# Loading 120 rows in place of 128 for the last matmul of an FFT convolution

## The chip, the cores and the metric

The kernel runs on one core of a Trainium2 chip. The metric is the device time of one execution in microseconds (us). The kernel before took 1574.06 us (median of 3 runs, 1570.44 to 1580.28).

## The reference

Two stages. The first convolves `u = x*v` (4 batches, 11456 positions, 128 channels) causally with a filter that a small network makes of position embeddings, and multiplies the outcome by `x`. The second sends each of the 45824 rows to one of 8 experts of two layers (128 to 1024 to 128), if a score of the row is above zero.

```
u = x * v
Uf = np.fft.rfft(u, n=L, axis=1)
Hf = np.fft.rfft(h_filt, n=L, axis=0)
y = np.fft.irfft(Uf * Hf[None, :, :], n=L, axis=1)[:, :S, :]
return (x * y).astype(np.float32)
...
e_idx = np.argmax(logits, axis=1)
...
    h = np.maximum(xc[mask] @ w1[e], 0.0)
    y[mask] = gate_w[mask, None] * (h @ w2[e])
out[do_compute] = xc + y
```

## The kernel before

The transform of length 3840 is split as 60 x 64 (`K1` = 60, `N2` = 64) and is done with matmuls in fp32 in three phases, one after the other in each engine's program.

- `first_phase` and `freq_phase`: the first takes the transform over 60 points (lines 209 and 211; its outcome is stored to DRAM from 120 partitions, line 197) and builds the filter (`filt`, line 257). The second takes the transform over 64 points (`spread`, L395), multiplies by the filter on VectorE and GpSimd, goes back over 64 points (`backer`, L430, 433) and stores the outcome `z` to the DRAM tensor `zd` (line 442). In `zd` each of the 32 output chunks has 2*`K1` = 120 rows (60 real, 60 imaginary) for either parity `p`, with 4 heads of 384 values (1536 bytes) each. Behind the last chunk lie 8 rows of zeros (`ZR`, line 1397), so that 128 rows can be read from every chunk.
- `out_phase`: for chunk `ch` and parity `p`, `load_z` reads rows of `zd` into the tile `zt` (two buffers, `ZB`). `load_z` is called from `produced` and, for the first two chunks, ahead of the loop, where the last head is loaded apart, as it is stored last. `product` multiplies `zt` by the table `c4`, for each of three blocks of a chunk: two matmuls (one for each `p`, into 64 PSUM partitions each) with 512 columns, then a product with `x` on VectorE (L1129). A matmul in fp32 stands as two instructions in the trace, so 32 x 3 x 2 products are 384 matmul instructions. The table's rows from 120 on are zero.
- The rest of `out_phase` decides for each row which expert it goes to, and the experts' work (`early_slots`, lines 735 to 825, afterwards `late_slots`) is put between the steps by a fixed order: the program's order on every engine is written out when it is built, and nothing of it depends on when a transfer lands.

The queues that matter: SP (SyncE) issues the loads of `zt` (L1109), of `x` (L1100, tile `ox`) and of `c4` (L1098) and the stores of the chunks (L1133), all in program order. ACT issues the stores of line 197 and the last twelve of line 442. GpSimd issues the indirect gathers and scatters of the experts.

Of the kernel before, what the change touches and what calls it, by code (L numbers as in the profile page):

```python
# [22 lines left out]
K1, N2 = 60, 64  # L23
# [4 lines left out]
NP = 4  # L28
# [25 lines left out]
C4 = 2  # L54
# [1000 lines left out]
def out_phase(tc, i, out, zd, ex, consts):  # L1055
# [3 lines left out]
    nc = tc.nc  # L1059
    NT = NS  # L1060
    NCH = H2
    with (
# [3 lines left out]
      with (  # L1066
# [23 lines left out]
        zs = zd.rearrange("p h r w -> r (p h) w")  # L1090
        c4s, xms, zx, zts, lgs = {}, {}, {}, {}, {}
# [11 lines left out]
        def load_z(ch, p, heads=slice(0, NP)):  # L1103

            if ch < NCH:
                if ch not in zts:
                    zts[ch] = oz.tile([128, 2 * NP, NS * DH], F32, name="zt")
                rows = slice(p * NP + heads.start, p * NP + heads.stop)
                nc.sync.dma_start(zts[ch][:, rows], zs[2 * K1 * ch:2 * K1 * ch + 128, rows])  # L1109

        def load(q, x=None):

# [7 lines left out]
        def product(ch, blk):  # L1120
            z, x = zx.pop(NB * ch + blk)
            if blk == 0:
                xms[ch] = ob.tile([128, NS, W], F32, name="xm", bufs=XM)
            xm = xms[ch]
            s = slice(blk * B, (blk + 1) * B)
            y = opy.tile([128, NP, B, DH], F32, name="y")
            for p in range(2):
                nc.tensor.matmul(y[p * 64:(p + 1) * 64], c4s[ch // C4][:, ch % C4, p, :], z[:, NP * p:NP * (p + 1)], start=True, stop=True)  # L1128
            nc.vector.tensor_tensor(xm[:, s, 0:D].rearrange("p b (h d) -> p h b d", h=NP), y, x, ALU.mult)  # L1129

        def store(ch, blk):
# [158 lines left out]
        for p in range(2):  # L1290
            load_z(0, p, most)
        ahead = [load_x(q) for q in range(ZT - 1)]
        for p in range(2):
            load_z(1, p, most)
        for ch in range(2):
            for p in range(2):
                load_z(ch, p, last)
# [37 lines left out]
        def produced(ch, blk):  # L1335
            product(ch, blk)
            load(NB * ch + blk + ZT - 1)

            if blk == NB - 1:
                load_z(ch + ZB, 0)  # L1340
            elif blk == 0 and ch > 0:
                load_z(ch + 1, 1)
# [128 lines left out]
```

## Time and profile before

| | us |
|---|---|
| median of 3 runs | 1574.06 |
| the profiled execution | 1575.11 |
| span of its instructions | 1573.2 |
| TensorE busy | 1485.4 |
| VectorE busy | 1057.4 |
| GpSimd busy | 963.8 |
| ScalarE busy | 790.3 |

Busy time is the time in which an engine had an instruction in work. A matmul's end is modelled in the profile, so that a busy TensorE is not TensorE at its peak. The granted clock is the share of TensorE's full speed that the chip allowed. The DMA share is the mean busy share of the core's 16 DMA engines; it can come out a little above 1. "Idle before" names the instruction or transfer that ended an engine's wait, "issue" a wait that nothing in the profile explains.

### The profile page before, as it was taken

The numbers are of one execution on the slowest core, as the hardware profiler recorded it, in microseconds if no ns is written. First come the engines' busy times: TensorE is split into PE (matmuls) and PEld (weight loads), VectorE is DVE, ScalarE is ACT, GpSimd is POOL, SyncE is SP. The second block draws the span as 40 slices with busy tenths as digits, with TensorE's granted clock in tenths as the row PEclk, the third lists the DMA queues.
The fourth block names the chain that finished last, engine by engine and source line by source line (L and its number), as shares of the span: only waits on it lengthen the run. The fifth ranks groups of instructions, "written<-read, shape, count | busy, mean of one in ns | idle before, by whom it ended". The sixth has DMA issues, their size and how long they took to land. (4 is left out here: it accounts for less than half of the span.)

```text
span 1573.2 us, 27965 instructions
## 1 busy us (share of the span) xinstructions
PE 1485.4 (94%) x9149; PEld 906.7 (58%) x9149; DVE 1057.4 (67%) x2356; ACT 790.3 (50%) x1643; POOL 963.8 (61%) x808
## 2 busy tenths in 40 slices
PE   6994999999999999978899999999979999999997
PEld 2552344444444444424477667666667788888887
DVE  1322776777777798856876666676658677777773
ACT  4552555555555544424355544544535455555554
POOL 0101876777777666621466369528856678888765
PEclk9996999999999999989899999999999999999999
DMA  8999999999999989969977687777521111111100
GB/s 319 316 335 339 364 390 371 377 360 363 359 390 361 301 230 359 316 218 344 314 237 227 218 240 243 246 233 234 152 57 39 36 46 45 46 45 44 41 28 24
DMA packets 199256, 362.18 MB, mean 230 GB/s; under 512 B 64476, under 2 KB 138730, under 8 KB 199070
## 3 DMA queue, kind: packets, MB, share of 16 engines
q1 hardware_dynamic: 173430, 272.15, 51.2%
q10 hardware_dynamic: 10192, 52.51, 9.1%
q0 software_dynamic: 15488, 35.74, 8.1%
q8 instruction: 73, 1.20, 0.3%
q14 instruction: 73, 0.60, 0.1%
HBM read 216.89 MB, written 145.42 MB: 230 GB/s over the span
## 5 line engine op out<-in xcount | busy, mean ns | idle before, releaser
L741 POOL DMA_INDIRECT out<-o,ids x182 | 197.7, 1086 | 158.2 <-DVE o L748 121.4
L488 POOL TENSOR_TENSOR y<-y,p 128x1536 f32<-128x1536 f32 x59 | 203.6, 3451 | 99.3 <-DVE p L415 99.3
L430 PE MATMUL ps<-y,c 64*128 64x256 f32 (+1 forms) x1440 | 259.2, 490 | 4.1 <-ACT wf L211 2.6
L670 POOL DMA_INDIRECT xt<-out,ids x182 | 189.6, 1042 | 48.1 <-issue 28.2
L883 DVE SCALAR_TENSOR_TENSOR hh<-hp,hh 128x1024 fp32r<-128x1024 f32 (+1 forms) x124 | 150.0, 1210 | 84.3 <-ACT hh L882 75.5
L430 PEld LDWEIGHTS ps<-y,c 64*128 64x128 f32 x1440 | 138.9, 187 | 117.3 <-issue 83.0
L399 ACT COPY xx<-xp 128x480 f32<-128x480 f32 x240 | 112.9, 523 | 129.2 <-PE xp L395 97.5
L882 ACT ACTIVATE hh<-hp 128x1024 fp32r<-128x1024 f32 (+1 forms) x124 | 127.6, 1029 | 94.7 <-issue 50.5
L433 ACT COPY z<-ps 128x512 f32<-128x512 f32 x240 | 103.7, 482 | 138.7 <-PE ps L430 127.2
L415 DVE TENSOR_TENSOR p<-xp,xx 128x768 f32<-128x768 f32 x240 | 169.3, 747 | 0.0
L415 DVE TENSOR_TENSOR y<-xp,xx 128x1152 f32<-128x1152 f32 x120 | 162.8, 1357 | 4.1
L406 DVE TENSOR_TENSOR xx<-xp,xx 128x384 f32<-128x384 f32 x120 | 66.7, 556 | 128.6 <-ACT xx L399 128.6
L395 PE MATMUL xp<-x,wf 128*64 128x480 f32 x512 | 120.9, 595 | 19.4 <-DMA x<-x1d 15.9
L1128 PE MATMUL y<-zt,c 128*64 128x512 f32 x384 | 109.2, 634 | 18.2 <-issue 10.5
L825 PEld LDWEIGHTS bank<-wd,h 128*128 128x128 f32 x896 | 104.2, 191 | 32.8 <-issue 25.9
L643 POOL MEMSET idle<- 128x512 f16 x226 | 122.5, 542 | 0.3
L209 PE MATMUL ps<-wf,c 60*120 60x384 f32 x512 | 119.4, 530 | 3.2 <-DVE wf L192 2.7
L211 ACT COPY wf<-ps 120x384 f32<-120x384 f32 x256 | 111.2, 499 | 21.6 <-PE ps L209 12.6
L192 POOL TENSOR_TENSOR wf<-wf 124x768 f32<-124x768 f32 x45 | 81.9, 1819 | 65.1 <-DVE xx L406 35.2
L621 POOL DMA_INDIRECT lists<-pl,lies x32 | 51.4, 1605 | 114.3 <-DVE step L1226 52.6
L825 PE MATMUL bank<-wd,h 128*128 128x128 f32 x896 | 114.5, 281 | 1.3 <-DVE o L748 1.3
L1129 DVE TENSOR_TENSOR xm<-y,ox 128x512 f32<-128x512 f32 x96 | 66.2, 689 | 69.1 <-PE y L1128 51.1
(180 smaller groups left out, 2934.3 us busy)
## 6 DMA issues: line engine op xcount, KB each, us to landing
wf<-xv SPq DMA_DIRECT2D x64, 768.0 KB
x1d<-wf ACTq DMA_DIRECT2D x64, 720.0 KB
x<-x1d SPq DMA_DIRECT2D x60, 768.0 KB
zt<-zd SPq DMA_DIRECT2D x60, 768.0 KB
zd<-z SPq DMA_DIRECT2D x108, 384.0 KB
out<-xm SPq DMA_DIRECT2D x96, 258.0 KB
ox<-xo SPq DMA_DIRECT2D x96, 256.0 KB
x1f<-fx POOLq DMA_DIRECT2D x16, 720.0 KB
```

The costliest lines, as they stand in the source:

```text
L209: nc.tensor.matmul(ps[p], self.c1[rows], u[rows, q * RUN:(q + 1) * RUN], start=True, stop=True)
L395: nc.tensor.matmul(xp[p * 64:(p + 1) * 64, c, 0:(NS + NB) * DH], c2(n % PER * KS + k)[:, c * 64:(c + 1) * 64], x1[:, k], start=True, stop= ...
L399: nc.scalar.copy(xx[:, 2 * c, 0:w], xp[:, c, 0:w])
L415: nc.vector.tensor_tensor(o[:, :, j].rearrange("p v m b d -> p v (m b) d"), v[:, :, None, s * DH:(s + 1) * DH].broadcast_to([128, NV, m, DH]),
L430: nc.tensor.matmul(zps[p], c3[r, v], yv[r, v, :, lo:hi], start=(v == 0), stop=(v == NV - 1))
L488: nc.gpsimd.tensor_tensor(y[:, :, :, 1:], y[:, :, :, 1:], p1, ALU.add)
L643: self.nc.gpsimd.memset(self.idle, 0.0)
L670: ins = nc.gpsimd.indirect_dma_start(out=xt[:, j], out_offset=None, in_=self.rows[0:have], in_offset=bass.IndirectOffsetOnAxis(ap=ids[:, j ...
L741: ins = nc.gpsimd.indirect_dma_start(out=self.rows, out_offset=bass.IndirectOffsetOnAxis(ap=ids[:, j:j + 1], axis=0), in_=o, in_offset=Non ...
L825: nc.tensor.matmul(bank[:, j * D:(j + 1) * D], h[f // nf][:, k:k + 128], wd[u][:, f * D:(f + 1) * D], start=(f == 0), stop=(f == F // 128 ...
L882: nc.scalar.activation(v[:, 0], hp, AF.Relu)
L883: nc.vector.scalar_tensor_tensor(v[:, 1], hp, 0.0, v[:, 0].bitcast(F32), ALU.max, ALU.subtract)
```

## The change

`load_z` reads 120 rows for each chunk into partitions 0 to 119 of `zt`, and both operands of the product are cut to partitions 0 to 119. The tile keeps its 128 partitions, and the table is still loaded whole.

```
-                nc.sync.dma_start(zts[ch][:, rows], zs[2 * K1 * ch:2 * K1 * ch + 128, rows])
+                nc.sync.dma_start(zts[ch][0:2 * K1, rows], zs[2 * K1 * ch:2 * K1 * (ch + 1), rows])
...
-                nc.tensor.matmul(y[p * 64:(p + 1) * 64], c4s[ch // C4][:, ch % C4, p, :], z[:, NP * p:NP * (p + 1)], start=True, stop=True)
+                nc.tensor.matmul(y[p * 64:(p + 1) * 64], c4s[ch // C4][0:2 * K1, ch % C4, p, :], z[0:2 * K1, NP * p:NP * (p + 1)], start=True, stop=True)
```

## Rows read from the trace of the kernel before

**Rows 1.** The page's 40 slices of the span, busy share in tenths.

```profile
PE   6994999999999999978899999999979999999997
DMA  8999999999999989969977687777521111111100
```

**Rows 2.** Stretches: length, busy PE, PEld, DVE, ACT, POOL; clock, DMA share, GB/s.

```profile
680.00:720.00 40.00, 27.36 (x163) 11.63 (x165) 19.06 (x42) 9.72 (x28) 2.55 (x2) 0.83 0.81 278
720.00:760.00 40.00, 33.94 (x315) 16.24 (x315) 31.94 (x136) 15.82 (x57) 6.40 (x6) 1.00 1.03 353
760.00:800.00 40.00, 35.23 (x295) 22.45 (x293) 29.83 (x120) 17.89 (x50) 22.34 (x27) 0.87 0.85 263
800.00:1128.00 328.00, 323.95 (x2757) 226.33 (x2750) 217.17 (x828) 161.17 (x421) 214.78 (x255) 1.00 0.75 233
```

**Rows 3.** Waits from 690 to 1140 us: us in total, times, longest.

```profile
PE y L1128 <- issue: 10.5, 2, 9.8
PEld y L1128 <- DMA zt<-zd: 1.9, 3, 1.0
DVE xm L1129 <- DMA zt<-zd: 2.7, 1, 2.7
SPq L1109 <- DMA zd<-z: 12.6, 3, 9.8
```

**Rows 4.** Timeline where the out phase begins: start, us, instruction, [idle before].

```profile
689.95 1.78 ACTq L442 DMA_DIRECT2D zd<-z  x2
...
696.64 2.04 SPq L1109 DMA_DIRECT2D zt<-zd  x4
...
699.04 2.35 PE L1128 MATMUL y<-zt,c 128*64 128x512 f32 x3 [9.84 <-issue]
```

**Rows 5.** Matmuls by line: ns min/median/max, first and last start, a form.

```profile
L430 PE MATMUL ps<-y,c x1440: 373/587/790, 164.3 to 688.8; 64*128 64x512 f32 x120, 64*128 64x256 f32 x60
...
L257 PE MATMUL ps<-hw,cf x160: 587/589/687, 35.1 to 116.9; 64*120 64x512 f32 x160
...
L209 PE MATMUL ps<-wf,c x512: 480/483/993, 11.2 to 537.7; 60*120 60x384 f32 x171
...
L1128 PE MATMUL y<-zt,c x384: 592/643/1116, 699.0 to 1128.0; 128*64 128x512 f32 x192
```

**Rows 6.** Timeline of TensorE: how closely matmuls of a line follow each other.

```profile
301.58 2.74 PE L430 MATMUL ps<-y,c 64*128 64x512 f32 x12
...
306.01 0.91 PE L209 MATMUL ps<-wf,c 60*120 60x384 f32 x4
...
709.94 1.08 PE L1128 MATMUL y<-zt,c 128*64 128x512 f32 x4
```

**Rows 7.** DMA issues of two lines: ns min/median/max of the issuing instruction.

```profile
L1109 SPq DMA_DIRECT2D zt<-zd x68: 333/426/1220, 679.0 to 1101.9; - x68
...
L197 ACTq DMA_DIRECT2D x1d<-wf x64: 322/323/730, 15.8 to 539.3; - x64
```

**Rows 8.** DMA from 680 to 760 us: packets and volume, then issues with KB each.

```profile
DMA packets 14869, 25.23 MB, mean 315 GB/s; under 512 B 1207, under 2 KB 9911, under 8 KB 14861
...
zt<-zd SPq DMA_DIRECT2D x13, 768.0 KB
...
zt<-zd SPq DMA_DIRECT2D x3, 576.0 KB
zt<-zd SPq DMA_DIRECT2D x4, 192.0 KB
```

**Rows 9.** DMA from 720 to 1128 us: packets and volume, then the issues of zt.

```profile
DMA packets 69218, 101.22 MB, mean 248 GB/s; under 512 B 13976, under 2 KB 44826, under 8 KB 69165
...
zt<-zd SPq DMA_DIRECT2D x56, 768.0 KB
```

**Rows 10.** DMA from 200 to 500 us: engines' share, then ACT's queue (line 197).

```profile
200.00:500.00 300.00, 296.75 (x1542) 127.68 (x1544) 221.74 (x317) 167.51 (x392) 230.25 (x98) 0.99 1.01 371
...
q10 hardware_dynamic: 4724, 25.81, 21.7%
```

## The prediction

> **What bounds the kernel now.** I read the slices first: TensorE is busy nine tenths or more nearly everywhere, and the DMA engines are full only up to the middle of the span [rows 1]. The change touches line 1109 and the two matmuls of line 1128, and the latter run only from 699 to 1128 us [rows 5], so I cut that part into stretches [rows 2]. The reader should see two different regimes there. From 800 to 1128 us TensorE is busy 323.95 of 328 us with the DMA engines at 0.75: work of the experts fills every gap, and TensorE sets the pace. From 720 to 760 us, before the experts' work begins, TensorE is busy 33.94 of 40 us and the DMA engines stand at 1.03: transfers have nothing to spare. From 680 to 720 us the phase begins, with 12.6 us of idle TensorE.
>
> Next, who really waits for the loads of z? From 690 to 1140 us TensorE's weight loads waited 1.9 us for them and VectorE 2.7 us, 4.6 us together [rows 3]. The one long wait is at the start: the last stores of z were issued from 689.95 us on, SP issued the loads of the last head at 696.64 us, and the first product followed at 699.04 us after 9.84 us of idleness [rows 4]. SP's longest wait there, 9.8 us, was for a store of z to land [rows 3]. That wait is for a store, whose size does not change.
>
> **The change part by part.** It removes rows 120 to 127 of each load, one sixteenth of 64 x 768 KB = 50.3 MB, that is 3.15 MB. It moves nothing in any program: the same loads and matmuls are issued in the same order, with the same waits, so nothing new is queued behind anything on SP or elsewhere.
>
> *Matmuls.* 384 instructions contract 120 rows instead of 128, still over 512 columns. No row shows 120 rows, so I take the nearest on both sides. With 64 rows, 256 columns take at least 373 ns (the minimum of line 430 is that of its smaller form) and 512 columns 587 ns (line 257): 214/256 = 0.836 ns per column. The matmuls of line 209 contract only 60 rows over 384 columns: the line gives 373 + 128 x 0.836 = 480 ns, and the minimum is 480. With 128 rows and 512 columns line 1128 takes 592 ns against 587 with 64 [rows 5]. So time goes by columns, and rows have no price: 0 us. If it went by rows, one sixteenth of 384 x 0.592 us would be 14 us, but line 209 would then be far below its line. The bound above comes from how closely matmuls follow each other. Twelve of line 430 take 2.74 us, (2.74 - 0.587)/11 = 0.196 us apart; four of line 1128 take 1.08 us, (1.08 - 0.592)/3 = 0.163 us apart; four of line 209, (0.91 - 0.480)/3 = 0.143 us for 384 columns, or 0.191 scaled to 512 [rows 6]. If cutting the rows took line 1128 from the spacing of a full column of the array to that of the partial ones, it would cost 384 x 0.033 = 12.7 us, all on the path, since TensorE is full. I take 0: those two lines also load 120 and 128 weight columns where line 1128 loads 64, which explains them as well. Weight loads have the same 64 columns: 0.
>
> *Issue on SP.* 68 instructions of 333 ns at least (426 in the median) [rows 7]. The stores of line 197 already have 120 rows and are issued in 322 to 323 ns [rows 7]. So 0; SP has time between issues anyway.
>
> *Transfers.* How much sooner does a load land? Upper bound of the gain: every byte saved is time saved. At the 353 GB/s of the full stretch [rows 2], 3.15 MB are 8.9 us over the whole phase. But a saving counts only where transfers hold something up. In 680 to 760 us z makes 13 x 768 + 3 x 576 + 4 x 192 = 12480 KB = 12.8 MB of 25.2 MB [rows 8]; a sixteenth is 0.80 MB, 2.3 us. Behind 800 us TensorE covers it, and what was waited for in all is 4.6 us [rows 3]. At the start the four loads of the first heads run ahead of the last store: a sixteenth of 4 x 576 KB is 0.15 MB, 0.4 us. So the likely gain lies between 0 and some 2 us if the saving is shared by all engines, with the ceiling at 8.9. Lower bound (a loss): loads that take longer in their new form, the third rival below. I take 0: 120 rows can be spread as 15 engines with 8 rows each, and then the engines that do work carry exactly what each of 16 carried for 128 rows, and only one is relieved. The nearest row for this form: line 197's 120-row stores, on ACT's queue, took 21.7% of engine time for 25.81 of 111.32 MB (23%: 371 GB/s x 300 us), with all engines at 1.01 [rows 10]. The form costs no more per byte than the rest and leaves no engine idle for long.
>
> [...]
>
> **Sum.** 0 (matmuls) + 0 (issue) + 0 (transfers) = 0. The profiled execution took 1575.11 us, 1.05 us above the median of the runs, so the sum is 1575.1 against that execution, and 1574 against the median.
>
> **The rivals.**
>
> *Saved bytes count everywhere.* Transfers follow the volume, and the full stretch and the start shrink: -2.3 - 0.4 us, about 1571; at the ceiling 1565. For: 1.03 in 720 to 760 us. Against: only 4.6 us of waits on z, and engine-wise nothing is saved. Chance 0.11.
>
> *Matmuls follow each other less closely.* +12.7 us, 1587. For: the spacing of lines 209 and 430. Against: the durations, which know no rows. Chance 0.05.
>
> *Loads of 120 rows run slower* (slower than before). The place is the stretch from 704 to 760 us: z is 12.8/25.2 = 51% of its volume, and the engines are full. A load that takes f times as long costs 56 x 0.51 x (f - 1) us: with f = 1.3 that is 8.6 us, and it decides (1%, 15.7 us) from f = 1.55 on; with 1.6 it gives 1591. Beyond 800 us z is 56 x 768 KB = 44.0 of 101.2 MB [rows 9], an estimated 0.33 of the engines' time at 0.75; this stays hidden until f = 1.76. Against: line 197's price per byte; but those are stores, and no row shows a load into 120 partitions. Chance 0.06.
>
> *The split uses only 8 engines* (120 = 8 x 15). From 720 to 1128 us the DMA share is (40 x 1.03 + 40 x 0.85 + 328 x 0.75)/408 = 0.79; z is 0.435 of it by volume [rows 9], 0.34, the rest 0.45. On half the engines z would be 0.34 x 15/16 x 2 = 0.64, together 1.09: 408 us become 445, +37 us, 1611. Against: the engines at 1.01 with 21.7% of their time in 120-row stores [rows 10]; on 8 engines these would have left the other 8 idle for twice that share. Chance 0.03.
>
> *The change does less than it says*, for instance since 128 rows' worth of work stays: the same time as the forecast.
>
> **How the numbers follow.** The forecast, within some 5 us of no change, has 0.72; the last 0.03 are for the clock. [...] The prediction is 1574. About 1% (15.7 us) is what a measurement of this kernel can tell from no change. Faster by over 1%, under 1558, needs more than the ceiling of saved bytes: 0.04, for what I don't see. Slower by over 1%, over 1590: slow loads (0.05), 8 engines (0.03), spacing with something on top (0.03), the rest (0.01): 0.12. Within 1%: 0.84. The range goes from the ceiling of the saving, 1565, to the bound of the spacing and of f near 1.5, 1588.
>
> **What would show it.** Right: line 1128 still at 592 ns at least and 0.163 us apart, with 120 rows in its form; zt with 720 KB per issue and waits on it of a few us; the DMA share from 800 to 1128 us down by a sixteenth of z's part, 0.02; TensorE's stretch from 800 us on as long as before. Wrong by the rivals: fewer idle us from 700 to 760 and an earlier last line 1128 (bytes); 1.21 us for four matmuls (spacing); long waits of line 1128 on zt from 704 to 760 us (slow loads), or everywhere (8 engines). If the time moves by over 1% and none of these rows moved, my reading of what bounds the phase is wrong.

## The result and the profile after

The changed kernel is slower: 1592.85 us (median of 6 runs) against 1577.77 us for the kernel before in runs beside it, ratio 1.0135 with a 95% interval of 1.0111 to 1.0159. This ratio is the one on record; the quotient of the two medians is 1.0096, so the size of the loss is known less closely than the interval says. The forecast was 1574 us and no change, with a range up to 1588. The profiled execution took 1593.7 us, its span 1591.9, 18.7 us more than that of before.

The programs of the engines are the same but for the form of lines 1109 and 1128. So the first question is when the time is lost. The timeline gives the moment at which VectorE multiplies the first block of each chunk (line 1129):

| chunk | before, us | after, us | after is late by |
|---|---|---|---|
| 0 | 702.4 | 704.8 | 2.5 |
| 3 | 724.7 | 733.4 | 8.7 |
| 5 | 742.1 | 756.4 | 14.3 |
| 7 | 761.4 | 781.7 | 20.3 |
| 9 | 788.8 | 811.3 | 22.5 |
| 15 | 879.0 | 901.6 | 22.6 |
| 31 | 1119.1 | 1141.5 | 22.4 |

The lines behind the row of chunk 9, before first:

```profile
788.77 0.69 DVE L1129 TENSOR_TENSOR xm<-y,ox 128x512 f32<-128x512 f32 x1 [2.81 <-PE y L1128]
```

```profile
811.26 0.69 DVE L1129 TENSOR_TENSOR xm<-y,ox 128x512 f32<-128x512 f32 x1 [2.81 <-PE y L1128]
```

All of it is lost up to chunk 9, and from there on not a tenth of a microsecond per chunk. Behind chunk 31, 3.7 us are won back; where, I did not follow. The stretches of the changed kernel (length, busy time of PE, PEld, DVE, ACT, POOL, clock, DMA share, GB/s), to be held against [rows 2]:

```profile
680.00:720.00 40.00, 25.27 (x137) 10.54 (x133) 16.87 (x35) 8.96 (x25) 3.67 (x3) 0.79 0.84 227
720.00:760.00 40.00, 32.58 (x234) 14.79 (x235) 22.34 (x87) 11.71 (x41) 2.97 (x3) 0.79 1.04 264
760.00:800.00 40.00, 28.52 (x230) 13.41 (x229) 26.58 (x120) 12.10 (x41) 15.83 (x19) 0.83 0.99 254
800.00:1100.00 300.00, 294.44 (x2508) 206.11 (x2509) 200.57 (x761) 149.75 (x389) 179.11 (x212) 0.99 0.91 229
```

From 720 to 760 us the DMA engines are as full as before (1.04), but they move 264 GB/s in place of 353. From 800 us on they are busy 0.91 of the time for 229 GB/s. The same stretch of the kernel before, and the share of SP's queue (packets, MB, share of the engines) in both, before first and after second:

```profile
800.00:1100.00 300.00, 296.47 (x2531) 207.57 (x2524) 199.31 (x754) 148.38 (x387) 189.43 (x224) 1.00 0.76 238
...
q1 hardware_dynamic: 44761, 64.44, 66.4%
```

```profile
q1 hardware_dynamic: 42580, 62.44, 81.2%
```

Fewer bytes take more engine time: 62.44 MB in 81.2% against 64.44 MB in 66.4%. If the 14.8% of 300 us, 44 us, are all put down to z, whose part before was some 0.33 x 300 = 99 us by volume, then z takes 143 us where a sixteenth less would be 93: an estimated 1.5 times as long per byte. The packets in the two traces say it directly: on SP's queue those of z are the ones of 1536 bytes, and from 800 to 1100 us one took 78.7 ns in the mean before and 115.5 after (1.47 times), from 704 to 800 us 74.9 and 113.6 (1.52 times). That is hidden here, as TensorE is busy 294.44 of 300 us; it is not hidden up to chunk 9.

The transfers of 680 to 760 us, for [rows 8], and waits for transfers from 690 to 1160 us, for [rows 3]:

```profile
DMA packets 11263, 19.65 MB, mean 246 GB/s; under 512 B 880, under 2 KB 7530, under 8 KB 11257
...
zt<-zd SPq DMA_DIRECT2D x10, 720.0 KB
```

```profile
PE y L1128 <- DMA c<-c: 3.0, 1, 3.0
...
PEld y L1128 <- DMA zt<-zd: 4.0, 4, 1.5
...
DVE xm L1129 <- DMA ox<-xo: 5.7, 4, 2.2
```

In the same 80 us, 10 whole loads of z are issued instead of 13, and now line 1128 waits 3.0 us for the table c4 too, and VectorE 5.7 us for x: other loads are late too. Most of the new waiting stands as "issue", for which the profile names no releaser. Line 1128 has the following from 704 to 812 us, where the kernel before had 2.6 us of weight loads and 0.7 us of matmuls waiting so; that these are waits for loads is inferred from l_alone below:

```profile
PEld y L1128 <- issue: 15.2, 9, 5.0
PE y L1128 <- issue: 13.7, 4, 4.7
```

And the matmuls themselves (min/median/max in ns, then a group of four from the timeline), for [rows 5] and [rows 6]:

```profile
L1128 PE MATMUL y<-zt,c x384: 592/643/1117, 701.1 to 1150.4; 120*64 120x512 f32 x192
```

```profile
889.75 1.08 PE L1128 MATMUL y<-zt,c 120*64 120x512 f32 x4
```

592 ns and 1.08 us for four: not a nanosecond has changed.

### The profile page after: what moved, and what is told of

It reads as the page before. It is cut to its first block, busy times and chain, and to the rows that moved or that the text cites. A ratio compares the mean times of both kernels' runs of the same rounds, so it can differ in the third digit from the quotient of the medians.

```text
span 1591.9 us, 27965 instructions
## 1 busy us (share of the span) xinstructions
PE 1490.7 (94%) x9149; PEld 906.2 (57%) x9149; DVE 1058.3 (66%) x2356; ACT 790.7 (50%) x1643; POOL 964.2 (61%) x808
## 5 line engine op out<-in xcount | busy, mean ns | idle before, releaser
L399 ACT COPY xx<-xp 128x480 f32<-128x480 f32 x240 | 112.9, 523 | 129.9 <-PE xp L395 96.9
L1128 PE MATMUL y<-zt,c 120*64 120x512 f32 x384 | 117.0, 668 | 30.4 <-issue 25.0
L395 PE MATMUL xp<-x,wf 128*64 128x480 f32 x512 | 120.9, 595 | 18.4 <-DMA x<-x1d 14.8
L825 PEld LDWEIGHTS bank<-wd,h 128*128 128x128 f32 x896 | 104.2, 191 | 32.8 <-issue 25.9
```

The lines of the kernel that those rows point to most:

```text
L395: nc.tensor.matmul(xp[p * 64:(p + 1) * 64, c, 0:(NS + NB) * DH], c2(n % PER * KS + k)[:, c * 64:(c + 1) * 64], x1[:, k], start=True, stop= ...
L825: nc.tensor.matmul(bank[:, j * D:(j + 1) * D], h[f // nf][:, k:k + 128], wd[u][:, f * D:(f + 1) * D], start=(f == 0), stop=(f == F // 128 ...
L1128: nc.tensor.matmul(y[p * 64:(p + 1) * 64], c4s[ch // C4][0:2 * K1, ch % C4, p, :], z[0:2 * K1, NP * p:NP * (p + 1)], start=True, stop=True)
```

## The experiments

Each ratio is against the kernel before on the same chip, with a 95% interval. "Chunk 0 to 9" is the time from the first product of chunk 0 to that of chunk 9, 86.4 us before and 106.4 us after; in five kernels whose early loads of z and x go into all 128 partitions (before, m_alone, z_heads, late120, store128) it lies between 86.4 and 90.0 us, so a single profile tells differences from some 4 us on.

| run | what is different from before | ratio | chunk 0 to 9, us |
|---|---|---|---|
| changed kernel | 120 rows loaded and contracted | 1.0135 (1.0111 to 1.0159) | 106.4 |
| m_alone | 120 rows contracted only | 1.0029 (1.0000 to 1.0058) | 90.0 |
| l_alone | 120 rows loaded only | 1.0152 (1.0106 to 1.0197) | 103.5 |
| late120 | 120 rows loaded from chunk 10 on, contracted in all | 0.9993 (0.9971 to 1.0014) | 87.9 |
| halves | z in two loads of 64 partitions | 1.0154 (1.0090 to 1.0219) | 107.6 |
| z_heads | z in two loads of half the heads | 1.0007 (0.9984 to 1.0030) | 88.4 |
| x_halves | x in two loads of 64 partitions | 1.0046 (1.0020 to 1.0071) | 96.3 |
| out_halves | output in two stores of 64 partitions | 1.0010 (0.9973 to 1.0046) | 91.2 |
| r112p8 | 120 rows as 112 and 8 | 1.0119 (1.0072 to 1.0165) | 102.2 |
| r112 | 112 rows only | one run | 96.9 |
| r96 | 96 rows only | one run | 104.9 |
| half_z | half of the heads from chunk 2 on | one run | 84.5 |
| mid64 | partitions 32 to 95 from chunk 2 on | one run | 84.0 |
| low64 | partitions 0 to 63 from chunk 2 on | one run | 85.8 |
| store128 | z stored from 128 partitions | 0.9976 (0.9952 to 1.0000) | 87.2 |

The runs that leave out part of z send rows to other experts, so their whole time says nothing, and they have no ratio; they are read only up to 1100 us.

### Which half of the change costs: m_alone and l_alone

m_alone keeps the loads and cuts the products:

```
-  c4s[ch // C4][:, ch % C4, p, :], z[:, NP * p:NP * (p + 1)]
+  c4s[ch // C4][0:2 * K1, ch % C4, p, :], z[0:2 * K1, NP * p:NP * (p + 1)]
```

> The loads stay at 128 rows; only the products are cut to 120 rows. If the loads are the cause (my theory now, after the trace of the changed kernel), the time is that of the kernel before, within 0.3%, and the first product of chunk 9 stays where it was, near 789 us. If the cut contraction costs anything of itself (its rival), the time lies above by up to the whole 15 to 19 us.

l_alone keeps the products and cuts the loads:

```
-  zts[ch] = oz.tile([128, 2 * NP, NS * DH], F32, name="zt")
+  zts[ch] = zbufs[ch % ZB]      # two fixed tiles, partitions 120 to 127 loaded with zeros once
...
-  nc.sync.dma_start(zts[ch][:, rows], zs[2 * K1 * ch:2 * K1 * ch + 128, rows])
+  nc.sync.dma_start(zts[ch][0:2 * K1, rows], zs[2 * K1 * ch:2 * K1 * (ch + 1), rows])
```

> The loads are cut to 120 rows; the products contract 128 (the eight partitions behind are filled with zeros once, and the two tiles of z stand fixed). If the loads are the cause: as slow as the changed kernel, ratio 1.010 to 1.016, 720 to 760 us at about 264 GB/s in place of 353, chunk 9 some 20 us late. If the contraction is: the time of before.

m_alone 1.0029 (its interval touches 1), l_alone 1.0152. Stretches of m_alone, then of l_alone:

```profile
720.00:760.00 40.00, 32.07 (x306) 15.86 (x308) 32.71 (x142) 14.23 (x53) 7.38 (x7) 0.96 1.00 333
```

```profile
720.00:760.00 40.00, 28.72 (x210) 12.34 (x208) 20.33 (x75) 12.03 (x41) 2.19 (x2) 0.91 1.05 259
```

333 GB/s with the old loads, 259 with the new ones: the loads are the cause. The cut contraction is in late120 too, for the whole phase, and that kernel is not slower.

### Where it costs: late120

```
+  n = 2 * K1 if ch >= 10 else 128
+  nc.sync.dma_start(zts[ch][0:n, rows], zs[2 * K1 * ch:2 * K1 * ch + n, rows])
```

> 128 rows for chunks 0 to 9, 120 rows from chunk 10 on; products on 120 rows. If slow loads cost time only while the DMA engines are full, that is up to chunk 9, they are hidden from chunk 10 on: ratio 0.998 to 1.003, DMA share from 800 us on near 0.9 in place of 0.75, and chunk 31 follows chunk 9 as before (some 330 us). If they cost time all along, two thirds of the loss stays: ratio 1.008 to 1.011.

0.9993, and the stretch from 800 us on is that of the changed kernel:

```profile
800.00:1100.00 300.00, 296.76 (x2521) 207.09 (x2520) 199.58 (x753) 148.93 (x387) 189.42 (x225) 1.00 0.92 232
```

The slow loads are all there (0.92 in place of 0.76), in two thirds of the chunks, and cost nothing. The whole price is paid up to chunk 9, where the DMA engines were full or nearly so before (0.81 to 1.03 in [rows 2]).

### Why the loads are slow: halves, z_heads, x_halves, out_halves

halves loads all 128 rows, but in two pieces; z_heads has as many pieces, cut along the heads:

```
+  for a, b in ((0, 64), (64, 128)):                                  # halves
+      nc.sync.dma_start(zts[ch][a:b, rows], zs[2 * K1 * ch + a:2 * K1 * ch + b, rows])
...
+  for a, b in ((rows.start, cut), (cut, rows.stop)):                 # z_heads
+      nc.sync.dma_start(zts[ch][:, a:b], zs[2 * K1 * ch:2 * K1 * ch + 128, a:b])
```

> All 128 rows as before, but each load issued as two, of partitions 0 to 63 and 64 to 127. Three theories of why 120 rows load slowly. Places: in a load of 120 rows each engine writes neighbouring partitions, so that several engines meet at one place of the SBUF, and each transfer slows down. [...] Under this theory the halves are as slow as the 120 rows or slower: below 280 GB/s from 720 to 760 us, the ratio at 1.01 to 1.02. Count: 120 rows leave one engine out. 64 rows can use all 16, so the halves would run like before, near 350 GB/s, ratio 1.00. Source: engines 8 rows apart in DRAM get in each other's way; in the halves they are 4 rows apart, and the ratio would be 1.00 too. More instructions on SP (64 issues more of 0.4 us) may add up to 2 us in every case.

> The control for the halves: 128 rows as before, each load issued as two, but of all 128 rows and half of the heads each, so the issues on SP are as many as in the halves. Places: engines and partitions are as in the kernel before, so ratio 1.000 to 1.003 and some 330 to 355 GB/s from 720 to 760 us. If the number of issues or of smaller transfers were what slows the halves: ratio 1.012 to 1.018 as there.

halves 1.0154, z_heads 1.0007. From 720 to 760 us, halves first:

```profile
720.00:760.00 40.00, 27.39 (x213) 12.46 (x212) 20.69 (x75) 11.98 (x42) 2.19 (x2) 0.96 1.08 258
```

```profile
720.00:760.00 40.00, 33.80 (x299) 16.40 (x299) 29.89 (x130) 14.25 (x51) 5.34 (x5) 0.96 1.03 347
```

258 GB/s with the engines full (1.08), though not a byte less is loaded than before and nothing in DRAM lies elsewhere; 347 with the same number of issues along the other dimension. So it is not the saved rows, not the count (one engine left out), by which the halves would have run like before, and not the issues. What 120 rows and the halves share is that fewer than all 128 partitions are written by one load; whether that is enough is asked further below.

x_halves and out_halves do the same to the two other large streams of the phase:

```
+  for a in (0, 64):                                                  # x_halves
+      nc.sync.dma_start(x[a:a + 64], i["xo"][ch, blk][a:a + 64])
...
+  for a in (0, 64):                                                  # out_halves
+      ex.store_rows(nc.sync.dma_start(out[ch][a:a + 64, s], xms[ch][a:a + 64, s]), ch)
```

> Loads of z as before; each load of x (tile ox, 256 KB, contiguous in DRAM) issued as two, of partitions 0 to 63 and 64 to 127. Places: it isn't about z or its layout in DRAM, any load into neighbouring partitions suffers. ox is a quarter of the volume in the full stretch (23 x 256 KB of 25.2 MB), half of z, so some 6 to 12 us lost up to chunk 9, ratio 1.004 to 1.008. Source (the layout of z in DRAM as the cause): ratio 1.000 to 1.003.

> Loads as before; each store of a block of the output (258 KB, as large as a load of x) issued as two, of partitions 0 to 63 and 64 to 127. If reading neighbouring partitions is as slow as writing them: lost time as with the halves of x, 3 to 10 us up to chunk 9, ratio 1.003 to 1.007. If only writing into the SBUF is slowed, which would explain why the stores of 120 rows ahead of the prediction showed nothing: no loss up to chunk 9, ratio 1.000 to 1.003.

x_halves loses 9.9 us up to chunk 9 and has 1.0046: a load that is contiguous in DRAM suffers too, so the layout of z is not needed for the loss. out_halves has 1.0010 with an interval on both sides of 1 and 4.8 us in its one profile, little more than the scatter. The packets show more. From 800 to 1100 us a packet of the output (2064 bytes) took 108.0 ns in the mean in place of 88.9, and one of x (2048 bytes) in x_halves 115.8 in place of 98.2. So these stores in halves are slowed about as much as these loads, and "only writing into the SBUF is slowed" does not hold. The loads of z suffer more than either (116.0 in place of 78.7 in halves); whether size or layout makes that difference is open.

### How many rows, or which partitions: r112p8, r112, r96, mid64, low64

```
+  for a, b in ((0, 112), (112, 120)):                                # r112p8
+      nc.sync.dma_start(zts[ch][a:b, rows], zs[2 * K1 * ch + a:2 * K1 * ch + b, rows])
...
+  nc.sync.dma_start(zts[ch][0:112, rows], zs[2 * K1 * ch:2 * K1 * ch + 112, rows])   # r112; r96: 96
```

> 120 rows in two loads, of 112 and of 8 rows, with the products on 120. Count: 112 rows use 16 engines with 7 each, so nearly all of the loss is gone, ratio 1.000 to 1.004. [...] Source: engines are 7 rows apart in place of 8, most of the loss stays or goes by chance.

> Only 112 rows of z are loaded and contracted; the last 8 rows are left out of the computation. Count (one engine left out): 16 engines with 7 rows, an eighth less than before, so from chunk 0 to chunk 9 no longer than before (86 us). [...]

> Only 96 rows of z are loaded and contracted; the last 24 are left out of the computation. Count and volume: 16 engines, a quarter less than before, chunk 0 to 9 at most the 86 us of before. [...]

r112p8 keeps most of the loss (1.0119; 102.2 us), where the count would have had 1.000 to 1.004. r112, with an eighth less to load than the kernel before, takes 96.9 us up to chunk 9, where the count would have had no longer than 86: a number of rows that divides by 16 does not bring the old time back. r96 takes 104.9 us. But TensorE ran that stretch at a lower clock (granted 0.67, and 0.59 from 760 to 800 us, where the kernel before had 1.00 and 0.87), and the DMA engines were not quite full (0.93 and 0.82). For all three kernels I had expected a smaller loss, by an estimate of mine that rests on nothing a run shows. The stretch of r112, then that of r96:

```profile
720.00:760.00 40.00, 33.71 (x270) 15.96 (x270) 27.46 (x114) 12.86 (x45) 4.31 (x4) 0.83 0.99 279
```

```profile
720.00:760.00 40.00, 37.92 (x258) 17.48 (x256) 25.82 (x103) 13.92 (x47) 4.30 (x4) 0.67 0.93 258
```

So the time up to chunk 9 can't be used for r96. From 800 to 1100 us TensorE's clock was 0.99 in r96, and there the packets of z can be compared: 96.8 ns in the mean in r112, 104.1 in r96, 115.5 in the changed kernel, against 78.7 in 128 partitions, that is 1.23, 1.32 and 1.47 times. What was still open is whether it matters which partitions are written. mid64 and low64 load the same number of rows and bytes with the same number of issues, into other partitions:

```
+  a, b = (0, 128) if ch < ZB else (32, 96)                           # mid64; low64: (0, 64)
+  nc.sync.dma_start(zts[ch][a:b, rows], zs[2 * K1 * ch + a:2 * K1 * ch + b, rows])
```

> From chunk 2 on only 64 of the 128 rows of z are loaded, into partitions 32 to 95 (the others keep the values of chunks 0 and 1, so the result is left wrong). Volume as with two of the four heads (half_z: DMA share 0.62 at 182 GB/s from 800 to 1100 us). [...] If any load of fewer than 128 partitions is slow: share above 0.72, as with low64.

> The same with partitions 0 to 63 in place of 32 to 95. [...] If only the number of partitions counts: the same share as mid64.

mid64 first, low64 second, from 800 to 1100 us, with SP's queue:

```profile
800.00:1100.00 300.00, 296.92 (x2512) 206.98 (x2511) 198.92 (x766) 148.07 (x387) 188.07 (x225) 1.00 0.63 184
...
q1 hardware_dynamic: 35031, 48.62, 52.4%
```

```profile
800.00:1100.00 300.00, 296.94 (x2522) 207.10 (x2520) 199.16 (x753) 148.82 (x387) 188.89 (x225) 1.00 0.70 185
...
q1 hardware_dynamic: 34608, 48.62, 59.6%
```

The same 48.62 MB take 52.4% of the engines' time into partitions 32 to 95 and 59.6% into 0 to 63. The DMA share is 0.63 and 0.70: the direction is clear, not the same share, as it would be if only the number of partitions counted, and the middle 64 cost hardly more than half of the heads in 128 partitions (half_z, 0.62). A packet of z took 86.0 ns in the mean in mid64, 109.1 in low64 and 81.1 in half_z. So a load with fewer than 128 partitions is not slow as such: it depends on which ones. That 0 to 63 would be the dearer ones I had expected; why they are, no run shows. Engines that meet at one place of the SBUF, the theory of the places, would be one reason, but neighbouring partitions alone are not enough for it, as 32 to 95 are neighbours too, and no trace here shows which engine writes where.

### What saved bytes would be worth: half_z

```
-  rows = slice(p * NP + heads.start, p * NP + heads.stop)
+  rows = slice(p * NP + heads.start, p * NP + (heads.stop if ch < ZB else 2))
```

> 128 rows as before, but from chunk 2 on only two of the four heads are loaded (the others keep the values of chunks 0 and 1, so the result is left wrong in them): half of the volume of z in the old form. It asks what saved bytes are worth in the full stretch. If transfers bind it: a quarter of the volume less, 60 us up to chunk 9 become 50 or less, chunk 0 to 9 in under 78 us. If the products' own chain on TensorE and VectorE binds it about as much: 82 to 88 us, and then a sixteenth could never have brought anything that can be measured.

```profile
720.00:760.00 40.00, 35.80 (x325) 17.59 (x324) 34.01 (x145) 14.93 (x55) 8.46 (x9) 0.96 0.83 267
```

With half of z gone the engines are no longer full (0.83), and chunk 0 to 9 takes 84.5 us in place of 86.4, less than the scatter. In the kernel before, transfers filled this stretch without holding it up, and a sixteenth less of z could not have been seen. That the products' own chain took about as long is inferred: TensorE is still busy only 35.80 and VectorE 34.01 of these 40 us.

### A version that might beat both: store128

The stores of z go from two times 64 neighbouring partitions. With `zd` laid out as (head, row of both parities), one store of 128 partitions takes their place:

```
-  for p in range(2):
-      eng.dma_start(zd[p, h, 0:H2 * 2 * K1]...[:, KS * k:KS * k + KS], z[p * 64:(p + 1) * 64]...)
+  eng.dma_start(zd[h, 0:2 * H2 * 2 * K1]...[:, KS * k:KS * k + KS], z...)
```

> Loads and products as in the kernel before; the DRAM tensor of z is laid out so that each chunk of z is stored in one transfer from 128 partitions, in place of two from 64 neighbouring ones (60 issues in place of 120). If stores from neighbouring partitions cost as much as loads into them, the DMA share of the second phase falls (below 0.95 from 500 to 650 us) and the last stores, for which SP waits 9.8 us before the out phase, land sooner: 1 to 5 us gained, ratio 0.997 to 0.999. If stores are hardly slowed, or TensorE sets the pace there: ratio 0.999 to 1.001.

> The kernel of store128 again, in more rounds: z stored from 128 partitions in one transfer. If the gain of the first runs holds: ratio 0.996 to 0.999, with an interval that ends below 1. If it was scatter: an interval around 1.

0.9976 (0.9952 to 1.0000) and, in a second measurement, 0.9974 (0.9943 to 1.0005). Both point to some 4 us less, and neither interval settles it. Two expected signs are absent: from 500 to 650 us the DMA share is 0.96 in both kernels, and SP's longest wait for a store of z is 13.0 us in place of 9.8. But the second phase is shorter: from the first to the last matmul of line 430 it takes 519.3 us in both profiles of store128, 524.5 in the kernel before and 521.1 to 526.2 in all other profiles, and from 650 to 680 us the DMA share is 0.53 and 0.56 in place of 0.77. So a gain is likely. Its cause is open, as the packets of 1536 bytes, nearly all of them stores of z, took hardly less time from 200 to 500 us (68.3 ns in the mean in place of 69.1).

## Why the prediction was wrong

**Matmuls, 0 us: right.** 592 ns and 1.08 us for four are unchanged, and m_alone and late120 show no cost that stands out of its interval. The rival of wider spacing is refuted; its sign should have been 0.592 + 3 x 0.196 = 1.18 us for four, where the prediction has 1.21.

**Issue on SP, 0 us: right.** 327 ns at least, 433 in the median, against 333 and 426 in [rows 7].

**Transfers, 0 us: wrong, and it decides.** The step that failed is the one that took 120 rows to be "15 engines with 8 rows each" that "carry exactly what each of 16 carried". No run shows over how many engines a load is spread; what they show is that equal bytes are not equal time: a packet of z of the same 1536 bytes took 115.5 ns in place of 78.7 from 800 to 1100 us (1.47 times), and 113.6 in place of 74.9 from 704 to 800 us (1.52 times). The row behind it [rows 10] was that of a store: line 197 reads the SBUF, line 1109 writes it. The prediction said itself that no row showed a load into 120 partitions, and yet set f = 1 by that row. Why the 120-row stores of line 197 showed no extra cost there is open: it is not that stores are spared in general, as out_halves slowed the output's by 1.21 times (88.9 to 108.0 ns).

Of the 18.85 us between 1574 and 1592.85, 3.7 us are not the change's: the kernel before itself has a median of 1577.77 us over six runs.

**The count of engines** does not account for the loss: 64 and 112 rows could be dealt evenly to 16 engines and 120 could not, yet from chunk 0 to chunk 9 halves took 107.6 us and r112 96.9, against 106.4 with 120 rows and 86.4 before.

**The third rival had mechanism, place and price.** It named the stretch from 704 us, the full engines and 56 x 0.51 x (f - 1): with f = 1.52 to 1.54 (the latter from 704 to 760 us, 114.9 ns for a packet of z in place of 74.6) that is 15 us, against the 20.0 us lost between chunk 0 and chunk 9. Its place is a little longer than 56 us, as the experts' work begins slowly up to chunk 9 (788.8 us). It also said that beyond 800 us the loads stay hidden up to f = 1.76, which late120 (0.92, and no loss) and the constant lag confirm. What failed was the chance of 0.06, and 0.12 for slower in all. Not in its price are the other packets of the stretch, which got slower beside the loads (from 704 to 800 us x from 96.4 to 104.2 ns, the output from 91.4 to 102.9), and the clock: from 720 to 760 us it was 0.79 in place of 1.00, and line 1128 was busy 40.77 us from 704 to 812 us against 31.68 us from 704 to 790 us before. TensorE waited more and ran at a lower clock. How much of the loss goes that way is not separated; halves lost as much with 0.96 in that stretch, but had 0.78 from 760 to 800 us, where the kernel before had 0.87. The 2.5 us at chunk 0 need not be the change's: before, m_alone, late120 and z_heads, whose first loads go into all 128 partitions, have chunk 0 anywhere from 694.6 to 704.0 us.

**The faster rival** (bytes saved count) is refuted by half_z: half of the bytes of z less from chunk 2 on brought 1.9 us of 86.4, less than the scatter. The reading that transfers "have nothing to spare" from 720 to 760 us was right, but the 1.03 did not mean that they set the pace: fewer bytes brought nothing that can be told from scatter, slower transfers cost 20.0 us.

## What to carry to other kernels

Before cutting a load to the partitions that are used, ask what the rest cost: here the time from chunk 0 to chunk 9 was 86.4 us with loads of all 128 partitions, 106.4 with 120, 96.9 with 112 and 107.6 with two times 64. Take the price of a form from a row of the same form and direction: here stores from 120 partitions showed no extra cost (21.7% of the engines' time for 23% of the bytes), and a packet of a load into 120 partitions took 1.5 times as long (115.5 ns in place of 78.7). And look by itself at a stretch where the DMA engines are full but hardly anybody waits for them, as here from 720 to 760 us (1.03): half of z less brought 1.9 us, less than the scatter, and slower loads cost 20.0.

## What the runs showed of the hardware

From 720 to 760 us all transfers together moved 327 to 353 GB/s where the loads of z went whole into 128 partitions (before, m_alone, late120, store128) and 347 where they were cut along the free dimension, but 258 GB/s where they were cut into partitions 0 to 63 and 64 to 127, and 259 to 264 where they went into 120 partitions, at a DMA share of 1.00 to 1.08 in each case. 64 partitions cost SP's queue 52.4% of the engines' time when they were 32 to 95, and 59.6% when they were 0 to 63, for the same 48.62 MB. A packet of 1536 bytes of z took 77.0 to 80.2 ns in the mean from 800 to 1100 us when written with all 128 partitions (before, m_alone, z_heads, store128), 86.0 into 32 to 95, 96.8 into the first 112, 104.1 into the first 96, 109.1 into 0 to 63, 115.5 into the first 120, and 116.0 in two halves.
